# Attention and MoE on one core: q and k of five batches turned by VectorE from doubled rows

## The chip, the core and the metric

The kernel runs on one core of one Trainium2 chip. The metric is the device time of one execution in microseconds (us). Inputs and output are float32 in device memory; the kernel computes with float16 operands and float32 sums. Engines are named as in the profile: PE (TensorE, matmuls), PEld (its weight loads), DVE (VectorE), ACT (ScalarE), POOL (GpSimd, which issues all loads), SP (which issues all stores).

## What is computed

Eight batches, eight heads, 576 tokens, 64 values a head. In the first four heads a token sees itself and the 31 tokens before it. In the last four it sees 32 tokens at distances 0, 4, 8 ... 124. The attention output of all heads, 4608 tokens by 512, then goes through two matrix products with a SiLU between them:

```python
    rel = pos[:, None] - pos[None, :]
    mask_plain = (rel >= 0) & (rel < window)
    mask_dil = (rel >= 0) & (rel < window * dilation) & (rel % dilation == 0)
...
    attn = attn / (np.sum(attn, axis=-1, keepdims=True) + 1e-09)
    return np.matmul(attn, v).astype(np.float32)
...
    h = x @ w_in
    g = h * (1.0 / (1.0 + np.exp(-h)))
    return (g @ w_out).astype(np.float32)
```

with w_in 512 by 2048 and w_out 2048 by 512.

## The kernel before

**Attention of a batch.** The four plain heads are called z=0 here (the prediction says first heads), the four dilated ones z=1 (second heads). In z=1 the tokens are split into four classes (token number modulo 4), and within a class the window is 32 neighbours, so both kinds work on blocks of 32 queries (`QB`) against 64 keys (`KB`): 18 blocks a head in z=0, 4 classes of 5 blocks in z=1.

1. `load_qk` (L113): POOL loads the rows of q and k into tile `n`, turned to float16 on the way: six DMAs a batch from batch 1 on (`load_one`, L97). The tile has two buffers for each of q and k. `load_v` (L120) loads v into `vw` (two buffers) by eight DMAs.
2. `transpose` (L219): PE turns the rows with the identity (L246), so that the 64 values of a head lie on partitions; for one batch 72 transposes in z=0 and 48 in z=1, half of them for k and half for q. They land in PSUM. DVE and ACT copy them into `kT`, `qT` (z=0, L250) and `kC`, `qC` (z=1, L258), which have two buffers each.
3. `scores` (L377): one matmul of 64 rows, 32 query columns as weights and 64 key columns as moving data for each block and head: 72 in z=0 (`score`, L273) and 80 in z=1 (`score_class`, L286). Head h writes partitions 32h to 32h+31 of the result, so four heads use four column groups of the array; the rows are 0 to 63 or 64 to 127. In z=0 the heads 0 to 3 use the row groups 0, 64, 64, 0. In z=1 the row group is the class modulo 2, and the order alternates it within a head, so eight places of the array follow one another. DVE then scales and adds the mask (L304) and takes the row maxima (L371).
4. `exps` (L431): ACT, 64 columns an instruction, with the sum (L451), 18 for z=0 and 20 for z=1.
5. `normal` (L464): DVE multiplies by the reciprocal of the sum into `pn` (L473). `turned` (L477): DVE transposes the probabilities in 32 by 32 blocks (L489); for batch 0 as 32-bit pairs of neighbouring columns, otherwise as 16-bit values.
6. `values` (L530): PE, matmuls of 32 rows with v as weights (L520), then `finish` (L546) copies the result into `xT` (L552, L554).

When pairs are turned, two neighbouring columns stay side by side. So batch 0 orders its keys in another way: `keys` (L263) takes the 64 keys as two halves of 32 and alternates between them, the mask of batch 0 is built in the same order, and `turned_cols` (L491) takes every second column for the product.

**MoE of a batch.** `layer1` (L596): 16 tiles of w_in columns, each 8 matmuls of 288 columns (L602) and a SiLU on ACT (L610). `layer2` (L659): row tiles of 128 tokens, 16 matmuls of 512 columns each (L671), copied by DVE to `ob` (L656, four buffers) and stored by SP. Two batches share nine row tiles: the even batch has four, the odd one five. Batch 0 goes in halves (L627, L647). Results of L602 and L671 lie in the PSUM pool `big`, which has two buffers, taken in turn; transposes, scores and products take the four buffers of the pool `ps`.

**The order** is written by hand. The MoE of batch b is the main line, and `plan_of` (L694) hangs the attention of the next two batches on its steps: steps 0 to 15 stand before the 16 tiles of layer 1, step 16 and each step after it before four matmuls of layer 2, and what is left comes at the end. For b from 2 on: step 0 normalizes batch b+1 z=0, its products are at step 6; step 10 has the scores of (b+1, z=1); step 13 the transposes of (b+2, z=0), step 17 its scores and step 18 its exponentials; step 27 the products of (b+1, z=1); step 31 the transposes of (b+2, z=1). `load_v(b+2)` and `load_qk(b+3)` are issued at step 16, in this order on POOL's queue. Batch 3's transposes stand elsewhere: z=0 at step 17 of b=1, z=1 at steps 1 and 3 of b=2. Each engine runs its own instructions in this order and waits on semaphores.

Of the kernel before, what the change touches and what calls it, by code (L numbers as in the profile page):

```python
# [8 lines left out]
F16 = mybir.dt.float16  # L9
F32 = mybir.dt.float32  # L10
BF16 = mybir.dt.bfloat16
U32 = mybir.dt.uint32
# [4 lines left out]
P = 128  # L17
W = 32
# [4 lines left out]
KB = 2 * QB  # L23
HF = P // 2
URS = (9, 12)


@with_exitstack
def kernel(
# [22 lines left out]
    NS = 512  # L52
    SA = NS // 2
    WM = 12

    ctx.enter_context(tc.manual_schedule())

# [31 lines left out]
    def tiles_qk(b):  # L89

        for which in (0, 1):
            t = nat.tile([P, 2 * sum(URS), D], F16, tag=f"n{which}", name=f"n{which}_{b}")
            u0, u1 = 2 * URS[0], 2 * (URS[0] + URS[1])
            qk[b, 0, which] = t[:, 0:u0].rearrange("p (h u) d -> p h u d", h=2)
            qk[b, 1, which] = t[0 : 2 * UPS[1] if b == 0 else P, u0:u1].rearrange("p (h u) d -> p h u d", h=2)

    def load_one(b, z, which):  # L97
# [8 lines left out]
        for i in (0, 1):  # L106
# [3 lines left out]
                in_=src[b, h : h + 2].rearrange("h (p u) d -> p h (u d)", u=URS[z]),  # L110
            )

    def load_qk(b):  # L113

        tiles_qk(b)
        for z in (1, 0) if b == 1 else (0, 1):
            for which in (1, 0):
                load_one(b, z, which)
# [75 lines left out]
    def build_mask():  # L194

        for n in (1, 2, 3):
            nc.vector.tensor_copy(band[n * W : n * W + W], band[0:W])
        nc.vector.tensor_copy(mask, band[:, None, :].broadcast_to([P, 10, KB]))
        nc.vector.memset(mask[:, 0:3:2, 0:W], NEG)

    first = mask[:, 2:10]

# [3 lines left out]
    def att(b):  # L206
        if b not in state:
            state[b] = {
                "qT": qTs[b % 2],
                "kT": kTs[b % 2],  # L210
                "qC": qCs[b % 2],
                "kC": kCs[b % 2],
                "vw": vws[b % 2],
                "pt": {},
                "xT": xtp.tile([P, HP, S], F16, tag="xT", name=f"xT_{b}"),
            }
        return state[b]

    def transpose(b, z, which, copies):  # L219
# [27 lines left out]
        for i in (0, 1):  # L247
# [3 lines left out]
            else:  # L251
                to_classes(a, which, i, ts[i].rearrange("d (e m) p -> d e m p", m=4), copies[i])

    def to_classes(a, which, i, t, copy):

        e, n = t.shape[1], t.shape[3]
        dst, i0 = ((a["qC"], 0), (a["kC"], W))[which]
        copy(  # L258
            dst[:, 2 * i : 2 * i + 2, :, i0 : i0 + n * e].rearrange("d h r (p e) -> d (h r) p e", e=e),
            t.rearrange("d e m p -> d m p e"),  # L260
        )

    def keys(b, t):  # L263

        return t.rearrange("d (x k) -> d k x", x=2) if b == 0 else t

    def score(b, h, j, dst, start=True):

        a = att(b)
        hp = h // 2  # L270
        o = (h + hp) % 2 * D
        r = slice(o, o + D)
        nc.tensor.matmul(  # L273
            dst[h * QB : h * QB + QB],
            a["qT"][r, hp, j * QB : j * QB + QB],
            keys(b, a["kT"][r, hp, j * QB : j * QB + KB]),
            start=start,
            stop=True,
            skip_group_check=not start,
        )  # L280

    def score_class(b, h, c, j, dst, start=True):

        a = att(b)
        r = slice(c % 2 * D, c % 2 * D + D)
        nc.tensor.matmul(  # L286
            dst[h * QB : h * QB + QB],
            a["qC"][r, h, c // 2, j * QB : j * QB + QB],
            keys(b, a["kC"][r, h, c // 2, j * QB : j * QB + KB]),
            start=start,  # L290
            stop=True,
            skip_group_check=not start,
        )
# [83 lines left out]
    def scores(b, z, half=None):  # L377

        a = att(b)
        if half != 1:
            a["s", z] = (
                [ps.tile([P, 8, KB], F32, tag="ps", name=f"s_{b}_{z}_{m}") for m in (0, 1)],
                [ps.tile([P, 2, KB], F32, tag="ps", name=f"ss_{b}_{z}_{m}") for m in range(1 + z)],
            )
        s, ss = a["s", z]
        n, cut = (NB, 8) if z == 0 else (NC, 3)
        js = range(0 if half != 1 else cut, cut if half == 0 else n)  # L390
        if z:
            for j in js:
                for e in (0, 1):
                    for h in range(HH):
                        for m in (0, 1):
                            dst = s[m][:, 4 * e + j] if j < 4 else ss[m][:, e]
                            score_class(b, h, 2 * e + m, j, dst)
        else:
            for j in js:
                for h in range(HH):  # L400
                    score(b, h, j, (*s, ss[0])[j // 8][:, j % 8])
        ms_ = {None: (0, 1), 0: () if z else (0,), 1: (0, 1) if z else (1,)}[half]
        for m in ms_:
            w = width(b, z, m)
            ms = msp.tile([P, WM, KB], F32, tag="ms", name=f"ms_{b}_{z}_{m}")
            if z:
                f = ms[:, 0:w].rearrange("p (r t) c -> p r t c", t=NC)
                masked(
                    f[:, :, 0:4].rearrange("p r t c -> p r (t c)"),
                    s[m].rearrange("p (r t) c -> p r (t c)", t=4),  # L410
                    first[:, 0:4].rearrange("p t c -> p (t c)")[:, None, :].broadcast_to([P, 2, 4 * KB]),
                )
                masked(f[:, :, 4], ss[m], band_of(2))
            elif m == 0:
                masked(ms[:, 0:8], s[m], first)
            else:
                masked(ms[:, 0:8], s[m], band_of(8))
                masked(ms[:, 8:10], ss[0], band_of(2))
            reduce_max(b, z, m, ms)
# [57 lines left out]
    def turned(b, z, hi):  # L477

        a = att(b)
        w = width(b, z, hi)  # L480
        key = z, hi * (b == 0)
        if key not in a["pt"]:
            a["pt"][key] = ptp.tile([P, DIL * NC, KB], F16, tag="pt", name=f"pt_{b}_{z}_{hi}")
        o = width(b, z, 0) * hi if b else 0
        out = a["pt"][key][:, o : o + w].rearrange("p t c -> p (t c)")
        src = a["pn", z, hi][:, 0:w].rearrange("p t c -> p (t c)")
        if b == 0:
            out, src = out.bitcast(U32), src.bitcast(U32)
        nc.vector.transpose(out, src)  # L489

    def turned_cols(b, pt, at, wd):  # L491

        if b:
            return pt[:, at : at + wd]
        at += at // QB % 2 * (1 - QB)
        if wd == QB:
            return pt[:, at : at + KB - 1 : 2]
        return pt[:, at : at + 2 * (KB - 1)].rearrange("p (t c) -> p t c", t=2)[:, :, 0::2]

    def products(b, z, part, c, j0, j1, dst):  # L500


        a = att(b)
        pt = a["pt"][z, part].rearrange("p t c -> p (t c)")
        o = (c % 2 * 2 + c // 2) * (j1 - j0) * KB
        for kb in range(max(j0 - 1, 0), j1):
            runs = []
            for j in (kb, kb + 1):
                if j0 <= j < j1:
                    key, x, col = dst(j)  # L510
                    at = o + ((j - j0) * 2 + kb - j + 1) * QB
                    if runs and runs[-1][0] == key and runs[-1][2] + QB == col:
                        runs[-1][4] += QB
                    else:
                        runs.append([key, x, col, at, QB])
            n = TL if z and kb == NC - 1 else QB
            for key, x, col, at, wd in runs:
                for h in range(HH):
                    r = slice(h * QB, h * QB + n)
                    nc.tensor.matmul(  # L520
                        x[h // 2][h % 2 * D : h % 2 * D + D, col : col + wd],
                        vws[b % 2][r, NB + kb * DIL + c if z else kb],
                        turned_cols(b, pt[r], at, wd),
                        start=(key, h) not in a["opened"],
                        stop=True,
                        skip_group_check=True,
                    )
                    a["opened"].add((key, h))
# [152 lines left out]

    def transposes(at, b, z, step, copies=both):
        for which in (1, 0):
            at(step, transpose, b, z, which, copies)

    def later(at, b, z, steps, copy=nc.vector.tensor_copy):
# [7 lines left out]
    def plan_of(b):  # L694
        ev = {}

        def at(s, fn, *args):
            ev.setdefault(s, []).append((fn, args))
# [44 lines left out]
        else:  # L743
            if b + 2 < B:
                at(16, load_v, b + 2)
            if b + 1 < B:
                if b == 2:
                    for n in (0, 1):
                        at(1 + 2 * n, transpose, 3, 1, 1 - n, both)
                later(at, b + 1, 0, (0, 0, 4, 6))  # L750
                if b + 3 < B:
                    at(16, load_qk, b + 3)
# [101 lines left out]
```

## Time and profile before

| what | value |
|---|---|
| runs | 315.74, 316.47, 316.49 us; median 316.47 |
| profiled execution | 316.89 us, of which the span from the first to the last instruction is 315.1 |
| DVE, share of the span | 60% |
| ACT | 69% |
| POOL | 24% |
| loads (queue q0) | 36704 packets, 18.61 MB, 45.6% of 16 engines' span |
| stores (queue q1) | 5328 packets, 9.44 MB, 8.2% |
| HBM | 37.21 MB read, 9.44 MB written |

The page gives busy time by engine, the chain of work that ended last, and groups of instructions: line, engine, operation, output and inputs with their shapes, count, then busy us and mean ns of one, then the idle time of the engine before them and what ended it. Busy time of matmuls counts overlapping ones once, so the mean of one (193 ns for a transpose) is far more than what each adds. The chain in order of time and the timeline give start and length of merged pieces; the length of a timeline piece runs to the end of its last instruction, so what a piece costs its engine is read from its start to the start of the next.

### The profile page before, as it was taken

The page shows a single profiled execution, that of the slowest core. Times are in us where ns is not written, and L with a number is a line of the kernel's source. Part 1 is how long each engine was busy: PE and PEld are TensorE (multiplying, and loading weights), DVE is VectorE, ACT ScalarE, POOL GpSimd, SP SyncE. Part 2 cuts the span into 40 slices and gives each one's busy share as a digit, 9 for nine tenths or more (in the row PEclk, how much of TensorE's full clock was granted, in tenths as well). Part 3 has the DMA queues.
Part 4 walks back from the last instruction along what each step waited for, and adds up shares of the span by engine and source line. Part 5 has one row for each costly group of instructions (what it writes and reads, how often), then busy time and mean ns, then how long its engine had stood idle before and what let it go on. Part 6 is the DMA issues. An engine that isn't in the chain of part 4 may idle for free.

```text
span 315.1 us, 11529 instructions
## 1 busy us (share of the span) xinstructions
PE 303.0 (96%) x5051; PEld 193.9 (62%) x5051; DVE 189.4 (60%) x356; ACT 218.6 (69%) x722; POOL 75.7 (24%) x127
## 2 busy tenths in 40 slices
PE   2799999999999999999999999999999999999995
PEld 2468654677446774577644775467745786467544
DVE  2866689445899667875585755883587552730011
ACT  2588688766998569974896568984899458736300
POOL 8826276634005400370008200150000000000000
PEclk9999999999999999999999999999999999999999
DMA  6999999999115921495019900290011100110021
GB/s 113 171 207 208 205 147 196 254 104 139 51 67 102 160 42 36 95 149 92 4 68 139 183 14 2 95 120 4 2 68 36 69 2 3 67 69 0 2 100 67
DMA packets 42081, 28.77 MB, mean 91 GB/s; under 512 B 20928, under 2 KB 37552, under 8 KB 42032
## 3 DMA queue, kind: packets, MB, share of 16 engines
q0 software_dynamic: 36704, 18.61, 45.6%
q1 hardware_dynamic: 5328, 9.44, 8.2%
q8 instruction: 39, 0.64, 0.8%
q14 instruction: 10, 0.08, 0.1%
HBM read 37.21 MB, written 9.44 MB: 148 GB/s over the span
## 4 chain that ended last, share of the span: by engine, by line
PE 88%; ACT 4%; DVE 4%; DMA 2%; issue 1%; POOL 0%; ACTq 0%; POOLq 0%
PE h L602 36%; PE o L671 30%; PE h L627 6%; PE x L520 4%; PE o L647 4%; PE t L246 3%; ACT pe L451 3%; PE s L273 2%; PE s L286 2%; DMA n<-in_q_dram 2%; ACT xT L554 1%; DVE pn L473 1%; DVE ob L656 1%; DVE pt L489 1%; DVE ms L304 0%
## 5 line engine op out<-in xcount | busy, mean ns | idle before, releaser
L602 PE MATMUL h<-xT,w_in 128*128 128x288 f16 x896 | 115.0, 286 | 0.1
L671 PE MATMUL o<-w_out,gT 128*128 128x512 f16 (+1 forms) x528 | 114.6, 373 | 0.0
L610 ACT ACTIVATE gT<-h 128x576 f16<-128x576 f32 x112 | 72.9, 651 | 56.7 <-PE h L602 55.8
L602 PEld LDWEIGHTS <-w_in 128*128 128x128 f16 x896 | 86.0, 98 | 23.9 <-issue 0.6
L671 PEld LDWEIGHTS <-gT 128*128 128x128 f16 x528 | 50.3, 98 | 54.4
L451 ACT ACTIVATE pe<-ms,nm 128x64 f32<-128x64 f32 x246 | 81.6, 335 | 0.1
L656 DVE COPY ob<-o 128x512 f32<-128x512 f32 (+1 forms) x35 | 23.5, 670 | 45.6 <-PE o L671 43.6
L451 ACT ACTIVATION_READ_ACCUMULATOR pe<-ms,nm 128x1 f32 x246 | 46.4, 189 | 0.0
L304 DVE SCALAR_TENSOR_TENSOR ms<-s,mask 128x512 f32<-128x512 f32 x28 | 19.2, 686 | 41.4 <-PE s L286 19.8
L126 POOL DMA_DIRECT2D vw<-in_v_dram x32 | 18.5, 586 | 105.6 <-PE x L520 102.4
L473 DVE TENSOR_TENSOR pn<-pe,r 128x640 f16<-128x640 f32 (+2 forms) x32 | 25.3, 792 | 1.1
L489 DVE STREAM_TRANSPOSE pt<-pn 128x640 f16<-128x640 f16 (+4 forms) x32 | 24.7, 772 | 1.1
L135 POOL DMA_DIRECT2D vw<-in_v_dram x32 | 21.2, 667 | 12.0 <-DMA w_out<-in_moe_w_out_dram 5.7
L371 DVE TENSOR_REDUCE nm<-ms 128x10 f32<-128x640 f32 (+1 forms) x28 | 22.0, 787 | 1.0
L627 PE MATMUL h<-xT,w_in 128*128 128x256 f16 (+1 forms) x128 | 18.3, 300 | 0.0
L520 PEld LDWEIGHTS <-vw 32*64 32x64 f16 (+1 forms) x1264 | 13.1, 107 | 7.7 <-issue 7.2
L554 DVE CAST xT<-x 128x288 f16<-128x288 f32 x24 | 16.3, 826 | 0.0
L520 PE MATMUL x<-pt,vw 32*64 32x64 f16 (+2 forms) x1264 | 15.0, 193 | 1.2 <-DVE pt L489 1.1
L627 PEld LDWEIGHTS <-w_in 128*128 128x128 f16 x128 | 12.7, 103 | 3.7
L647 PE MATMUL o<-w_out,gT 128*128 128x512 f16 x64 | 14.7, 380 | 0.2 <-ACT ob L656 0.2
L246 PEld LDWEIGHTS <-n 64*64 64x64 f16 (+1 forms) x912 | 11.0, 105 | 5.9 <-issue 4.8
L552 DVE CAST xT<-x 128x288 f16<-128x288 f32 x24 | 9.3, 449 | 8.0 <-PE x L520 8.0
(72 smaller groups left out, 224.5 us busy)
## 6 DMA issues: line engine op xcount, KB each, us to landing
out_dram<-ob SPq DMA_DIRECT2D x35, 256.0 KB, 2.0
n<-in_k_dram POOLq DMA_DIRECT2D x9, 288.0 KB, 5.7
n<-in_q_dram POOLq DMA_DIRECT2D x9, 288.0 KB, 6.7
vw<-in_v_dram POOLq DMA_DIRECT2D x31, 80.0 KB, 4.5
vw<-in_v_dram POOLq DMA_DIRECT2D x32, 72.0 KB, 4.1
w_in<-in_moe_w_in_dram POOLq DMA_DIRECT2D x4, 512.0 KB, 9.8
w_out<-in_moe_w_out_dram POOLq DMA_DIRECT2D x4, 512.0 KB, 11.1
n<-in_k_dram POOLq DMA_DIRECT2D x14, 144.0 KB, 7.2
```

The lines of the kernel that those rows point to most:

```text
L135: nc.gpsimd.dma_start(out=vw[h * QB : h * QB + QB, 0:NB], in_=v[b, h].rearrange("(m p) d -> p m d", p=QB))
L371: nc.vector.tensor_reduce(out=nm[:, 0:w], in_=ms[:, 0:w], axis=AX.X, op=ALU.max, negate=True)
L451: nc.scalar.activation(pe[:, t, :], src[t], AF.Exp, bias=a["nm", z, hi][:, t : t + 1], scale=k, accum_out=l[:, t : t + 1],)
L473: nc.vector.tensor_tensor(pn[:, 0:w], a["pe", z, hi][:, 0:w], r[:, 0:w, None].broadcast_to([P, w, KB]), ALU.mult)
L489: nc.vector.transpose(out, src)
L520: nc.tensor.matmul(x[h // 2][h % 2 * D : h % 2 * D + D, col : col + wd], vws[b % 2][r, NB + kb * DIL + c if z else kb], turned_cols(b, pt[ ...
L602: nc.tensor.matmul(h[:, half, 0:HS], w_in16[:, c, f * P : f * P + P], xT[:, c, half * HS : half * HS + HS], start=(c == cs[0]), stop=(c == ...
L610: nc.scalar.activation(gT[:, f, s0 : s0 + S].rearrange("p (a c) -> p a c", a=2), h[:, :, 0:HS], AF.Silu)
L627: nc.tensor.matmul(hs[i // m][:, i % m, 0 : c1 - c0], w_in16[:, c, (f + i) * P : (f + i + 1) * P], xT[:, c, c0:c1], start=(c == 0), stop=( ...
L647: nc.tensor.matmul(o, gT[:, f, t * P : (t + 1) * P], w_out16[:, f, :], start=(f == 0), stop=(f == NFF - 1),)
L656: copy(ob, o)
L671: nc.tensor.matmul(o[:, 0, 0:m], gT[:, f, t * P : (t + 1) * P], w_out16[:, f, cols], start=(f == 0), stop=(f == NFF - 1),)
```

## The change

From batch 3 on (`DT = 3`) q and k no longer go through PE. POOL loads them in blocks of 32 rows on 32 partitions: for z=0's q each row is a token, 32 values at a time; for the others each row is a pair of neighbouring tokens, of which 96 values are taken. A second copy, 32 columns on in device memory, goes to the next 32 partitions, and the other two heads to the upper 64 partitions: four DMAs for each of k z=0, q z=0, k z=1, q z=1. DVE turns each of the four in one instruction of 1152 16-bit values a partition (`turn_qk`), straight into the tiles `qT`, `kT`, `qC`, `kC`, where even and odd tokens now lie in two planes. The calls stand at the steps where the transposes of that batch stood; both of (3, z=1) are at step 1 of b=2.

The scores of these batches read through `turned_q` and `turned_k`. The row group is now that of the head (0 for heads 0 and 1, 64 for 2 and 3), and the heads follow in the order 0, 2, 1, 3; in z=1 the class is the outer loop.

The probabilities of all batches are turned as 32-bit pairs. Therefore all batches take their keys alternating between two halves, the mask in SBUF is built in that order, and all products read every second column.

The transposes of batches 1 and 2 stay on PE.

```diff
+DT = 3
...
-        nc.vector.tensor_copy(mask, band[:, None, :].broadcast_to([P, 10, KB]))
-        nc.vector.memset(mask[:, 0:3:2, 0:W], NEG)
+        pairs = mask.rearrange("p t (k x) -> p t k x", x=2)
+        nc.vector.tensor_copy(
+            pairs, band.rearrange("p (x k) -> p k x", x=2)[:, None].broadcast_to([P, 10, W, 2])
+        )
+        nc.vector.memset(pairs[:, 0:3:2, :, 0], NEG)
...
     def load_qk(b):
 
         tiles_qk(b)
+        if b >= DT:
+            for z in (0, 1):
+                for which in (1, 0):
+                    u, e = (1, QB) if z == which == 0 else (2, GW)
+                    n = HH // 2 * S // u // QB
+                    for half in (0, 1):
+                        for x in (0, 1):
+                            o = half * HF + x * QB
+                            nc.gpsimd.dma_start(
+                                out=turned_rows(b, which, z)[o : o + QB],
+                                in_=bass.AP(
+                                    (q, k)[which].tensor,
+                                    (b * H + z * HH + half * HH // 2) * S * D + x * QB,
+                                    [[u * D, QB], [u * QB * D, n], [1, e]],
+                                ),
+                            )
+            return
...
+    def turn_qk(b, z, which):
+        n = HH // 2 * MG
+        if which == 0 and z == 0:
+            nc.vector.transpose(
+                att(b)["qT"].rearrange("p a c -> p (a c)"), turned_rows(b, 0, 0).rearrange("p g t -> p (g t)")
+            )
+            return
+        o = which * (1 + z) * QB
+        src = turned_rows(b, which, z)
+        nc.vector.transpose(
+            planes(b, z, which)[:, :, o : o + n * QB].rearrange("p r (g t) -> p r g t", t=QB),
+            src.rearrange("p g (r t) -> p r g t", t=QB)[:, 0:3:2],
+        )
...
     def keys(b, t):
 
-        return t.rearrange("d (x k) -> d k x", x=2) if b == 0 else t
+        return t.rearrange("d (x k) -> d k x", x=2)
+
+    def turned_q(b, z, h, c, j):
+        r = slice(h // 2 * D, h // 2 * D + D)
+        if z == 0:
+            return att(b)["qT"].rearrange("p a c -> p (a c)")[r, h % 2 * S + j * QB : h % 2 * S + j * QB + QB]
+        o = h % 2 * HS + j * KB + c // 2
+        return planes(b, 1, 0)[r, c % 2, o : o + KB - 1 : 2]
+
+    def turned_k(b, z, h, c, j):
+        r = slice(h // 2 * D, h // 2 * D + D)
+        if z == 0:
+            o = h % 2 * HS + (j + 1) * QB // 2
+            return planes(b, 0, 1)[r, :, o : o + QB].rearrange("p r (x t) -> p t r x", x=2)
+        o = h % 2 * HS + j * KB
+        t = planes(b, 1, 1)[r, c % 2, o : o + 2 * KB].rearrange("p (x t y) -> p y t x", x=2, y=2)
+        return t[:, c // 2]
...
-                for e in (0, 1):
-                    for h in range(HH):
-                        for m in (0, 1):
-                            dst = s[m][:, 4 * e + j] if j < 4 else ss[m][:, e]
-                            score_class(b, h, 2 * e + m, j, dst)
+                for c, h in [(c, h) for c in range(DIL) for h in (0, 2, 1, 3)] if b >= DT else [
+                    (2 * e + m, h) for e in (0, 1) for h in range(HH) for m in (0, 1)
+                ]:
+                    e, m = c // 2, c % 2
+                    score_class(b, h, c, j, s[m][:, 4 * e + j] if j < 4 else ss[m][:, e])
...
-                for h in range(HH):
+                for h in (0, 2, 1, 3) if b >= DT else range(HH):
...
-        if b == 0:
-            out, src = out.bitcast(U32), src.bitcast(U32)
-        nc.vector.transpose(out, src)
+        nc.vector.transpose(out.bitcast(U32), src.bitcast(U32))
...
         for which in (1, 0):
+            if b >= DT:
+                at(step, turn_qk, b, z, which)
+                continue
             at(step, transpose, b, z, which, copies)
...
                 if b == 2:
-                    for n in (0, 1):
-                        at(1 + 2 * n, transpose, 3, 1, 1 - n, both)
+                    transposes(at, 3, 1, 1)
```

`planes` splits the tile into the two planes of even and odd tokens; `turned_rows` finds the loaded rows in tile `n`.

More of the change, by code (lines that the diff above doesn't have):

```diff
@@ L54 @@
     WM = 12
+    MG = S // KB
+    GW = 3 * QB
     ctx.enter_context(tc.manual_schedule())
@@ L91, in tiles_qk @@
         for which in (0, 1):
-            t = nat.tile([P, 2 * sum(URS), D], F16, tag=f"n{which}", name=f"n{which}_{b}")
+            t = nat.tile([P, H // 2 * MG * GW], F16, tag=f"n{which}", name=f"n{which}_{b}")
+            if b >= DT:
+                qk[b, which] = t
+                continue
+            t = t[:, 0 : 2 * sum(URS) * D].rearrange("p (u d) -> p u d", d=D)
             u0, u1 = 2 * URS[0], 2 * (URS[0] + URS[1])
@@ L111, in load_one, with turned_rows @@
             )
+    def turned_rows(b, which, z):
+        t, n = qk[b, which], HH // 2 * MG
+        if which:
+            return t[:, z * n * GW : (z + 1) * n * GW].rearrange("p (g e) -> p g e", e=GW)
+        if z == 0:
+            return t[:, 0 : n * KB].rearrange("p (g e) -> p g e", e=QB)
+        return t[:, n * KB : n * (KB + GW)].rearrange("p (g e) -> p g e", e=GW)
     def load_qk(b):
         tiles_qk(b)
+        if b >= DT:
[15 more added lines that the diff above has]
+            return
         for z in (1, 0) if b == 1 else (0, 1):
@@ L252, in transpose, with planes @@
                 to_classes(a, which, i, ts[i].rearrange("d (e m) p -> d e m p", m=4), copies[i])
+    def planes(b, z, which):
+        t = att(b)[(("qT", "kT"), ("qC", "kC"))[z][which]]
+        t = t.rearrange("p a c -> p (a c)") if z == 0 else t.rearrange("p a x c -> p (a x c)")
+        n = HH // 2 * MG * QB + (which * QB if z == 0 else (QB, 3 * QB)[which])
+        return t[:, 0 : 2 * n].rearrange("p (r c) -> p r c", r=2)
+    def turn_qk(b, z, which):
[11 more added lines that the diff above has]
+        )
     def to_classes(a, which, i, t, copy):
@@ L263, in keys @@
     def keys(b, t):
-        return t.rearrange("d (x k) -> d k x", x=2) if b == 0 else t
+        return t.rearrange("d (x k) -> d k x", x=2)
[7 more added lines that the diff above has]
+        r = slice(h // 2 * D, h // 2 * D + D)
+        if z == 0:
+            o = h % 2 * HS + (j + 1) * QB // 2
[3 more added lines that the diff above has]
+        return t[:, c // 2]
     def score(b, h, j, dst, start=True):
@@ L274, in score @@
             dst[h * QB : h * QB + QB],
-            a["qT"][r, hp, j * QB : j * QB + QB],
-            keys(b, a["kT"][r, hp, j * QB : j * QB + KB]),
+            turned_q(b, 0, h, 0, j) if b >= DT else a["qT"][r, hp, j * QB : j * QB + QB],
+            turned_k(b, 0, h, 0, j) if b >= DT else keys(b, a["kT"][r, hp, j * QB : j * QB + KB]),
             start=start,
@@ L287, in score_class @@
             dst[h * QB : h * QB + QB],
-            a["qC"][r, h, c // 2, j * QB : j * QB + QB],
-            keys(b, a["kC"][r, h, c // 2, j * QB : j * QB + KB]),
+            turned_q(b, 1, h, c, j) if b >= DT else a["qC"][r, h, c // 2, j * QB : j * QB + QB],
+            turned_k(b, 1, h, c, j) if b >= DT else keys(b, a["kC"][r, h, c // 2, j * QB : j * QB + KB]),
             start=start,
@@ L486, in turned, with turned_cols @@
         src = a["pn", z, hi][:, 0:w].rearrange("p t c -> p (t c)")
-        if b == 0:
-            out, src = out.bitcast(U32), src.bitcast(U32)
[L489 to L494, printed above, removed]
+        nc.vector.transpose(out.bitcast(U32), src.bitcast(U32))
+    def turned_cols(pt, at, wd):
         at += at // QB % 2 * (1 - QB)
@@ L522, in products @@
                         vws[b % 2][r, NB + kb * DIL + c if z else kb],
-                        turned_cols(b, pt[r], at, wd),
+                        turned_cols(pt[r], at, wd),
                         start=(key, h) not in a["opened"],
@@ L683, in transposes @@
         for which in (1, 0):
+            if b >= DT:
+                at(step, turn_qk, b, z, which)
+                continue
             at(step, transpose, b, z, which, copies)
```

## Prediction

> **What bounds the kernel now.** I read the page first, for the bound.
>
> ```profile
> PE 303.0 (96%) x5051; PEld 193.9 (62%) x5051; DVE 189.4 (60%) x356; ACT 218.6 (69%) x722; POOL 75.7 (24%) x127
> ...
> PE 88%; ACT 4%; DVE 4%; DMA 2%; issue 1%; POOL 0%; ACTq 0%; POOLq 0%
> ...
> L489 DVE STREAM_TRANSPOSE pt<-pn 128x640 f16<-128x640 f16 (+4 forms) x32 | 24.7, 772 | 1.1
> ...
> L246 PE MATMUL t<-ident,n 64*64 64x64 f16 (+1 forms) x912 | 13.2, 193 | 0.6 <-DMA n<-in_q_dram 0.4 <-issue 0.3
> ```
>
> That is the page: busy time by engine, the chain that ended last by engine, and two groups. TensorE (PE) is busy 96% of the span and 88% of the chain that ended last; from 20 us on it hardly idles. So each instruction that leaves PE shortens the run by its place in PE's sequence, and work added to DVE, ACT or POOL costs nothing until PE waits for it. Next the chain in order of time (start, us, line, count), for prices of such places:
>
> ```profile
> 111.75 3.04 PE h L602 x24
> 114.80 0.76 PE t L246 x72
> 115.56 3.04 PE h L602 x24
> ...
> 130.58 2.70 PE o L671 x12
> 133.28 0.70 PE t L246 x48
> 133.98 0.97 PE o L671 x4
> ...
> 257.56 6.00 PE h L602 x48
> ...
> 275.24 3.56 PE o L671 x16
> ```
>
> The 72 transposes split 48 matmuls of L602: 111.75 to 118.60 is 6.85 us, and the unbroken 48 took 6.00. They cost 0.85 us: their own 0.76, and the drain of one more change of matmul shape. In the same way 48 transposes cost 4.37 - 3.56 = 0.81.
>
> **Off PE: transposes of batches 3 to 7.** 600 of the 912. Batches 4 to 7 lose 0.85 + 0.81 each: 6.64. Batch 3's stand elsewhere: 77.62 to 82.35 is 4.73 us for 16 L671 and 72 transposes, and 16 without a break take 3.46 (275.17 to 278.63 in the timeline): 1.27. 99.20 to 106.20 is 7.00 for 48 L602 and two groups, against 5.88 in another batch: 1.12. Sum **-9.03 us**. The copies behind them (L250, L258; 0.75 us each on DVE, 0.64 on ACT) go too; PE does not wait for them, so that is room, not time.
>
> **Pairs in the transpose of the probabilities.**
>
> The groups with their shapes kept apart show both kinds (busy us, then mean ns):
>
> ```profile
> L489 DVE STREAM_TRANSPOSE pt<-pn 128x640 f16<-128x640 f16 x21 | 17.8, 845 | 0.7
> ...
> L489 DVE STREAM_TRANSPOSE pt<-pn 128x320 uint32<-128x320 uint32 x1 | 0.5, 511 | 0.0
> ```
>
> 640 halves (f16 values) turned as 320 pairs save 0.33 us each, 512 save 0.27 (711 to 445 ns). Three products (L520) on PE wait for this result, by their length against the same product elsewhere: 1.08 against 0.78 at 89.98, 0.96 against 0.81 at 96.34, 1.34 against 0.81 at 273.83. The first two go whole, since DVE has saved 0.60 and 1.27 us by then; of the third go the 0.33 us of its last transpose: **-0.78**. The products now read every second column; batch 0 does that already at full clock (24.96 to 27.9 us), in bunches of four every 31.6 ns, as at 164.6 without the step. Cost 0, and no bound to keep, since the trace shows the operation itself.
>
> **Added on DVE: four transposes of 1152 halves a batch.** No row has that size. The line through 512 (711 ns) and 640 (845) gives 1.38 us. Below, the pair rate gives 0.78 for 576 pairs; above, the slowest strided row of DVE, L554 with 826 ns for 288 elements, gives 3.3. I take 1.38: same operation, same type. Per batch DVE gets 4 x 1.38 - 4 x 0.75 - 1.27 = +1.25 us of about 36; the question is only where.
> - Step 13 (first heads): DVE ends the row maxima at 149.9 in batch 3's stage; two turns, 1.31 from start to start, end at 152.5. PE wants them for the scores at 154.22 - 0.87 = 153.35. Cost 0, cover 0.8 us.
> - Step 17 of batch 1: 77.83 + 2.6 = 80.4, wanted at 81.1. Cost 0. Step 1 of batch 2 ends ahead of the xT copies at 106.66. Cost 0.
> - Step 31 of batches with four row tiles (2 and 4) has no cover. DVE's timeline, start and us first:
>
> ```profile
> 130.42 2.72 DVE L554 CAST xT<-x 128x288 f16<-128x288 f32 x4
> 133.72 0.76 DVE L258 COPY kC<-t 128x576 f16<-128x576 f16 x1 [0.58 <-PE t L246]
> 134.39 0.75 DVE L258 COPY qC<-t 128x576 f16<-128x576 f16 x1
> 135.05 0.68 DVE L656 COPY ob<-o 128x512 f32<-128x512 f32 x1
> ```
>
> The output copy at 135.05 frees the PSUM buffer that the next batch's second L602 tile needs (`big` has two). Today it ends at 135.73 and PE gets there at 135.95. Changed: turns 133.07 to 135.69, the copy ends at 136.38, while PE gets there at 134.07 + 0.98 = 135.05. PE stands still for about 1.38 us, in two batches: **+2.75**. Batches 3 and 5 have a fifth row tile in the other buffer, 3.45 us of cover.
>
> **Loads.** A batch's q and k come by 16 DMAs of 576 or 1152 pieces (64 or 192 bytes written) in place of six: 11520 packets. The nearest rows are v's pieces of 128 bytes; the DMA view of 66 to 68 us, which holds almost only these, says
>
> ```profile
> DMA packets 1911, 0.25 MB, mean 123 GB/s; under 512 B 1888, under 2 KB 1911, under 8 KB 1911
> ```
>
> 955 packets a us, so a load takes 12 us. It is issued behind v from 100 us on and wanted at 149.6 (first heads) and 168. POOL issues for 16 x 0.66 us, and the next batch's v, queued behind, has 40 us. Output stores on SP's queue share the engines, but their four buffers are 3.4 us apart. Cost 0. The other bound is the rate of the old loads with 1152-byte packets, 161 a us (1771 in 104 to 115): too slow, see the rivals; 955 is nearer by size.
>
> **Scores.** This is the open term. Every key operand now alternates between columns 32 to 128 bytes apart (batch 0 already does), in batches 1 and 2 too. Batch 0 ran before 22.7 us, where 128x256 matmuls start every 213 ns and afterwards every 109: half clock, though the clock column prints 1.00 there.
>
> ```profile
> 10.27 0.70 PE L246 MATMUL t<-ident,n 64*64 64x64 f16 x36 [0.36 <-DMA n<-in_q_dram]
> ...
> 17.02 0.81 PE L273 MATMUL s<-kT,qT 64*32 64x64 f16 x40
> ...
> 18.72 0.61 PE L520 MATMUL x<-pt,vw 32*64 32x64 f16 x32
> ```
>
> That is the timeline of PE (start, us, line, count). All three stream 64 columns in bunches of four. By their single starts, a bunch takes 53.3 ns in the first (plain) and the third (step of two), and 61.7 in the scores. So the alternation already binds at half clock. At full clock a plain score bunch takes 29.3 ns. If the limit is a time of the memory, a bunch stays at 61.7; if it is 74 PE cycles against 64, it is some 33, as fast as instructions now arrive (8.2 ns each). More than 61.7 is unlikely: a faster PE doesn't slow the memory. I take 61.7, since a limit outside PE explains why a step of two costs nothing. First heads: 18 bunches + 0.12 of start = 1.23 us against 0.71, in seven batches: 3.64. Second heads: the new order (0, 2, 1, 3) cycles four places of the array instead of eight, so in batches 3 to 7 20 bunches + 0.12 = 1.35 against 0.74: 3.05; in 1 and 2 eight overlap and 61.7 is hidden by arrival (66). **+6.7**.
> The Trainium skill (Advanced Engine Details and Errata, SBUF Cachelines) speaks against this change: two consecutive reads must hit one 16-byte line to reach full rate. Read as halving the rate, it gives 58.7 ns a bunch and a sum 0.7 us lower than mine; no row at full clock shows it.
> The skill (TensorEngine Tiling, PSUM Pressure) also says that two row groups cannot write one PSUM bank at once, which the new order does. The first heads do it today, starting 3 ns apart; the trace disagrees.
>
> The mask's two operations at 28 us (0.49 us, at most 0.8) meet an idle DVE: 0.
>
> **Sum:** -9.03 - 0.78 + 2.75 + 6.7 = -0.36 us. The profiled run took 316.89 us (span 315.1), 0.42 above the median of 316.47; against that median the forecast is **316.1**.
>
> **Rivals.**
> - *The alternation costs cycles, not time.* Scores +0, sum -7.06: 309.4. For it: both clocks would show 10 extra cycles. Against: they appear only with the far step. 0.22; something between, near 312.8, 0.06.
> - *The turns are late* (slower). If 1152 halves over two planes take 2.0 us instead of 1.38, the standstill grows by 1.24 twice and step 13 loses its 0.8 us of cover and 0.45 more in four batches: +4.3, 320.4. It decides from about 1.7 us a turn. For it: DVE is nearly full from 82 to 106. Against: the runs are 32 halves long. 0.12.
> - *The loads come late.* From 100 us to the last turn of first heads, due at 221, POOL's queue has 36096 packets to move; below 298 a us PE waits. At 250 it would be 23 us late: 339. Against: 955 measured. 0.05.
> - *It does not do what it says* (transposes stay on PE): excluded by PE's instruction list, 1200 rows shorter.
>
> **Numbers.** Forecast 0.55. Its terms: scores 4.8 (a bunch of 53.3 ns, the plain one at half clock) to 6.7, standstill 0.4 (turns of 0.78) to 4.1 (turns of 1.7); both ends together give 311.9 and 317.4, its own range, with less of the low end, is 313.5 to 317.5. The likeliest case lies close to no change, and 0.3% (0.95 us) is what a measurement can tell: it splits 0.19 faster, 0.26 same, 0.10 slower. With the rivals: faster 0.47, same 0.26, slower 0.27. The range 309.0 to 318.5 leaves out the late turns and the late loads, and perhaps a tenth of the first rival's cases.
>
> **What would show it.** L246 falls from 912 to 312. The bunches of the score lines are the test: 72 scores near 1.2 us (this), near 0.7 (first rival). PE stands still near 135 and 208 us for the output copy. A turn's mean is 1.3 to 1.5 us. No DVE wait for a load. I am wrong if PE waits for DVE or POOL at the scores.

## The result and the profile after

| | before | changed |
|---|---|---|
| median, us | 316.48 (315.74 to 316.96, 4 runs) | 321.33 (320.87 to 322.13, 4 runs) |
| profiled execution, us (span) | 316.89 (315.1) | 320.87 (319.1) |

The ratio is 1.0158, 95% interval 1.013 to 1.0187: the change made the kernel slower, by some 4.9 us. The forecast was 316.1, its range 309.0 to 318.5.

The page of the changed kernel: busy time by engine, and the chain that ended last by engine.

```profile
PE 305.0 (96%) x4451; PEld 197.3 (62%) x4451; DVE 190.5 (60%) x354; ACT 208.3 (65%) x704; POOL 112.6 (35%) x177
...
PE 88%; DVE 5%; ACT 3%; DMA 2%; issue 1%; POOL 1%; DVEq 0%; POOLq 0%
```

PE has 600 matmuls fewer and is busy 2 us longer. So the instructions went, and the ones that stayed became dearer. The groups by line say which were asked of whom: PE's transposes, then DVE's new ones (busy us, mean ns).

```profile
L282 PE MATMUL t<-ident,n 64*64 64x64 f16 (+1 forms) x312 | 4.7, 201 | 1.1 <-DMA n<-in_q_dram 1.1
```

```profile
L309 DVE STREAM_TRANSPOSE kC<-n 128x1152 f16<-128x1152 f16 x5 | 6.9, 1379 | 0.0
...
L303 DVE STREAM_TRANSPOSE qT<-n 128x1152 f16<-128x1152 f16 x5 | 6.7, 1334 | 0.0
```

912 transposes became 312, and a turn takes 1.33 to 1.38 us: both as forecast. The chain (start, us, line, count) shows what did not come out. Before, the scores of the second heads of batch 3 and of the first heads of batch 4 stood there so:

```profile
111.00 0.61 PE s L286 x64
...
119.46 0.63 PE s L273 x64
```

The same stretch in the changed kernel, where the last 16 and the last 8 matmuls of a group have lines of their own:

```profile
110.95 1.21 PE s L364 x64
112.16 0.28 PE ss L364 x16
112.44 5.99 PE h L676 x48
...
119.29 1.88 PE s L351 x61
121.17 0.22 PE ss L351 x7
```

The 48 matmuls of layer 1 now run unbroken in 5.99 us (6.85 before): the gain is there. But from their first start to the start of what follows, the second heads' scores take 1.49 us (0.75 before; 1.35 forecast), and the first heads' 2.10 (0.71 before; 1.23 forecast). By single starts (of the single matmuls in the trace), a bunch of four first-head matmuls takes 111 ns; 18 bunches are 2.0 us.

The other loss forecast, the late output copy, is in DVE's timeline (start, us), and in PE's line behind it:

```profile
134.16 1.39 DVE L309 STREAM_TRANSPOSE kC<-n 128x1152 f16<-128x1152 f16 x1
135.47 1.33 DVE L309 STREAM_TRANSPOSE qC<-n 128x1152 f16<-128x1152 f16 x1
136.73 0.65 DVE L730 COPY ob<-o 128x512 f32<-128x512 f32 x1
```

```profile
137.43 5.06 PE L676 MATMUL h<-xT,w_in 128*128 128x288 f16 x40 [1.09 <-DVE ob L730]
```

The two turns stand ahead of the copy, and PE waits for it. From start to start PE loses 1.25 us here and 0.90 at 211, in the same place of a later batch, where the profile names ACT's gT as what it waited for. At 100.7 PE loses 0.27 us to an output copy that has the xT copies ahead of it, and no turn.

### The profile page after: what moved, and what is told of

It reads as the page before. It is cut to its first block, busy times and chain, and to the rows that moved or that the text cites. A ratio compares the mean times of both kernels' runs of the same rounds, so it can differ in the third digit from the quotient of the medians.

```text
span 319.1 us, 10398 instructions
## 1 busy us (share of the span) xinstructions
PE 305.0 (96%) x4451; PEld 197.3 (62%) x4451; DVE 190.5 (60%) x354; ACT 208.3 (65%) x704; POOL 112.6 (35%) x177
## 4 chain that ended last, share of the span: by engine, by line
PE 88%; DVE 5%; ACT 3%; DMA 2%; issue 1%; POOL 1%; DVEq 0%; POOLq 0%
PE h L676 34%; PE o L745 33%; PE s L351 4%; PE o L721 4%; PE h L701 3%; PE x L594 3%; PE s L364 2%; DMA n<-in_q_dram 2%; ACT pe L529 2%; DVE xT L628 1%; PE t L282 1%; ACT xT L628 1%; DVE ob L730 1%; POOL n L108 1%; DVE pn L551 1%
## 5 line engine op out<-in xcount | busy, mean ns | idle before, releaser
L676 PEld LDWEIGHTS <-w_in 128*128 128x128 f16 x896 | 86.4, 98 | 26.6 <-issue 2.7
L140 POOL DMA_DIRECT2D n<-in_q_dram x40 | 29.5, 765 | 1.1 <-PE x L594 0.8
L140 POOL DMA_DIRECT2D n<-in_k_dram x40 | 26.4, 683 | 6.6 <-DMA n<-in_k_dram 3.8
L701 PE MATMUL h<-xT,w_in 128*128 128x256 f16 (+1 forms) x128 | 17.3, 289 | 0.0
L628 DVE CAST xT<-x 128x288 f16<-128x288 f32 x24 | 16.3, 825 | 0.3 <-PE x L594 0.3
L565 DVE STREAM_TRANSPOSE pt<-pn 128x320 uint32<-128x320 uint32 (+2 forms) x32 | 15.8, 495 | 1.1
L351 PEld LDWEIGHTS <-qT 64*32 64x32 f16 x576 | 12.8, 104 | 4.4 <-issue 3.3
```

The source lines that it names most:

```text
L140: nc.gpsimd.dma_start(out=turned_rows(b, which, z)[o : o + QB], in_=bass.AP((q, k)[which].tensor, (b * H + z * HH + half * HH // 2) * S * ...
L351: nc.tensor.matmul(dst[h * QB : h * QB + QB], turned_q(b, 0, h, 0, j) if b >= DT else a["qT"][r, hp, j * QB : j * QB + QB], turned_k(b, 0, ...
L628: copy(a["xT"][:, 2 + hp].rearrange("d (i r) -> d r i", r=DIL)[:, 2 * e : 2 * e + 2], x.rearrange("d (r i) -> d r i", r=2)[:, :, 0:CL],)
L676: nc.tensor.matmul(h[:, half, 0:HS], w_in16[:, c, f * P : f * P + P], xT[:, c, half * HS : half * HS + HS], start=(c == cs[0]), stop=(c == ...
L701: nc.tensor.matmul(hs[i // m][:, i % m, 0 : c1 - c0], w_in16[:, c, (f + i) * P : (f + i + 1) * P], xT[:, c, c0:c1], start=(c == 0), stop=( ...
```

## The experiments

**Theory:** the loss lies in the order in which a score matmul reads its 64 key columns; the turned layout of k makes that order worse than the two-place alternation that I had priced. In batches 3 to 7 the first heads' tokens lie in two planes (even and odd tokens, 1216 bytes apart), and each plane gives two places 32 bytes apart, so one matmul takes its columns in turn from four places (stretches of memory that it reads on from), `[2,2,16]`, where batch 0 cycles through two, `[2,32]`. **Rivals:** the third level of the pattern costs, whatever it reads; the long distance costs; or PE waits for something else, such as the turned rows.

### Nine orders of the same reads (key_orders)

```diff
+            t = planes(b, 0, 1)[r, :, o : o + QB]
+            flat = att(b)["kT"].rearrange("p a c -> p (a c)")[r, o : o + KB]
+            if b == 3:
+                return t.rearrange("p r (x t) -> p r t x", x=2)
+            if b == 4:
+                return t.rearrange("p r (x t) -> p x r t", x=2)
+            if b == 5:
+                return t.rearrange("p r t -> p t r")
+            if b == 6:
+                return flat.rearrange("p (a t) -> p t a", a=4)
+            return flat.rearrange("p (x t y) -> p t x y", x=2, y=2)
```

(These are the first heads of batches 3 to 7; other orders stand likewise in batches 1 and 2 and for the second heads of batches 4 to 7.)

> Only the order changes in which the scores read their 64 key columns, another one in each batch (the keys then no longer meet the mask, so the output is not the attention's). First heads, 72 matmuls: batch 1 swaps neighbours two columns apart, batch 2 cycles eight places 16 bytes apart, batch 3 alternates two places 32 bytes apart under a third level, batch 4 reads runs of 16 under a third level, batch 5 alternates the two halves 1216 bytes apart in two levels, batch 6 cycles four places 32 bytes apart in two levels, batch 7 alternates two places 64 bytes apart after two adjacent columns each. Changed kernel: 2.09 us in batches 3 to 7 (four places, three levels, 32 and 1216 bytes apart), 1.21 in batches 1 and 2 (two places). Theory 'places' (the number of places cycled sets the price): batch 3 1.23, batch 4 0.7, batch 5 1.23, batch 6 2.1, batch 7 0.7 to 1.23, batch 1 0.7, batch 2 2.1 or more. Rival 'levels' (a third level of the pattern sets it): batches 3, 4 and 7 2.1, batches 5, 6 and 2 1.23. Rival 'distance' (the 1216 bytes set it): batches 3, 6, 7 at most 1.23, batch 4 about 0.8, batch 5 2.1. Second heads, 80 matmuls, 1.49 in the changed kernel: batch 4 without alternation (step of two), batch 5 with query columns side by side, batch 6 with both plain, batch 7 with the heads in the order 0 to 3. If the key order sets their price too, batches 4 and 6 take 0.75 and 5 and 7 1.49; if the query's step of two adds the part above 1.35, batch 5 takes 1.35.

The chain's lines of the scores (start, us; first heads L371, second heads L384; the last 8 or 16 matmuls of a group have lines of their own, 0.07 to 0.28 us, left out here, and some records are missing from the counts):

```profile
67.08 1.88 PE s L371 x64
...
82.30 1.10 PE s L371 x58
...
118.75 0.63 PE s L371 x64
...
145.36 0.61 PE s L384 x61
...
152.96 1.10 PE s L371 x64
...
182.29 1.21 PE s L384 x62
190.62 1.89 PE s L371 x54
...
225.88 0.67 PE s L371 x64
```

In order of time: batch 2 (eight places), 3 (two places, three levels), 4 (runs of 16, three levels), the second heads of 4 (no alternation), 5 (two places 1216 bytes apart), the second heads of 5 (query side by side), 6 (four places, two levels), 7 (two places in runs of two). The whole groups take 2.11, 1.23, 0.71, 0.75, 1.23, 1.49, 2.11 and 0.75 us. Batch 1, which swaps neighbours inside 8 bytes, keeps 29 ns a bunch. So neither the levels (1.23 and 0.71 with three, 2.11 with two) nor the distance (32 or 1216 bytes: 1.23) sets the price. With one column at each visit the number of places does: one place takes 29 ns a bunch, two 62, four and eight 111; with two columns at each visit two places take 36 (batch 7). The query's step and the order of the heads (batch 7's second heads, 1.49) cost nothing. With these reads the profiled run took 315.2 us.

### One plane for the first heads' keys (key_rows)

```diff
-                    u, e = (1, QB) if z == which == 0 else (2, GW)
+                    u, e = (2, GW) if z else (1, QB)
...
-            return planes(b, 0, 1)[r, :, o : o + QB].rearrange("p r (x t) -> p t r x", x=2)
+            return keys(b, att(b)["kT"].rearrange("p a c -> p (a c)")[r, o : o + KB])
```

> The first heads' k of batches 3 to 7 is loaded like their q, one token in a piece of 32 values, so that their keys lie in one plane and the scores alternate between two places instead of four; 1152 pieces more in each such load. Theory 'places' or 'distance': 72 scores fall from 2.09 to 1.23 us in five batches, 4.3 us, 317.0 against 321.3. If the four places are not what costs (a wait of another kind, such as PE waiting for the turned rows), no change: 321.3. If more pieces make loads late: slower than 321.3.

317.50 us, 1.0032 [1.0019, 1.0045] against before; 3.8 below the changed kernel, where 4.3 was expected. The line that answers to 1.88:

```profile
119.20 1.09 PE s L350 x64
```

So four places instead of two cost the change nearly 4 us in the time of the whole run too. Of the half microsecond that is missing, 0.35 is the second standstill, 1.25 us here (at 208) in place of 0.90; the added pieces of load cost nothing that shows.

### Each half of the change alone (plain_keys, pairs_only)

plain_keys has DVE's turns, the loads of key_rows, and keys in order (its main lines):

```diff
-        return t.rearrange("d (x k) -> d k x", x=2)
+        return t.rearrange("d (x k) -> d k x", x=2) if b == 0 else t
...
-        nc.vector.transpose(out.bitcast(U32), src.bitcast(U32))
+        if b == 0:
+            out, src = out.bitcast(U32), src.bitcast(U32)
+        nc.vector.transpose(out, src)
```

> As the run with one plane, and all key operands but batch 0's are read in order again (a step of two in the second heads of batches 3 to 7), so the probabilities of batches 1 to 7 are turned as halves. It is the first part of the change alone, without the pairs. Theory that the alternation is the loss: first heads 0.71 in seven batches, second heads 0.75: from 321.3 down by 6.9 (batches 3 to 7) + 1.0 (1 and 2) + 3.8 (second heads) and up by 0.8 for the three waits on the turned probabilities: 310.4, below both kernels. Rival that DVE becomes the bound, now that it has both the turns and the slower transposes (1.4 us a batch more): 314 or more, with PE waiting for DVE at 90 to 100 us.

pairs_only is the changed kernel with `DT = 8`:

> The second part alone: q and k of all batches are turned by PE as before, the probabilities as pairs, and all keys alternate between two places. First heads 1.21 in seven batches against 0.71 (+3.5), second heads 0.80 against 0.74 (+0.4), three waits on the turned probabilities gone (-0.8): 316.5 + 3.1 = 319.6 by the theory that the alternation is the loss; 315.7 if only the turned layout's keys lose.

plain_keys: 310.84 us, 0.9821 [0.9807, 0.9836]. pairs_only: 319.28, 1.0087 [1.0067, 1.0107]. The turns of q and k alone are a gain of 5.5 us; the pairs alone a loss of 2.9, since the transposes that they shorten are DVE's, off the path but for 0.8 us, while the order that they force on the keys is paid by PE. The first heads' scores of batch 4 in plain_keys, without their last 8:

```profile
117.31 0.63 PE s L346 x64
```

and in pairs_only, behind the second heads' of batch 3 without their last 16:

```profile
111.75 0.67 PE s L364 x64
...
120.27 1.09 PE s L351 x60
```

The 80 scores of the second heads take 0.81 us in pairs_only, with keys from two places, and 0.75 in plain_keys, with keys in order and the new order of heads; with both they take 1.49. By single starts, pairs_only has eight matmuls on eight places of the array side by side in 62 to 66 ns; the changed kernel, whose layout has one row group for each head, has four in 69. So 0.68 of the 0.74 us that the second heads lose comes from the two together: slower reads, and half as many of them at a time.

DVE, busy 199.0 us in plain_keys, did not become the bound.

### The late output copy (moved, plain_moved, plain_moved_b2)

```diff
-                if b == 2:
-                    transposes(at, 3, 1, 1)
+                transposes(at, b + 1, 1, 5)
...
-            if b + 2 < B:
-                transposes(at, b + 2, 1, 31)
```

> The changed kernel with the second heads' turns of batches 3 to 7 taken from step 31 (step 1 of batch 2's stage for batch 3) to step 5 of the stage that uses them, behind the output copies and ahead of 4 us in which DVE idles. Theory that the two turns ahead of the output copy hold PE up: the standstills of 1.25 and 0.90 us and a wait of 0.27 at 100.7 go, 321.3 - 2.4 = 318.9. Rival, the wait only moves (PE then waits at the second heads' scores, about 147 us, for the turns): 320.5 to 321.5.

319.24 us (1.0102 [1.0079, 1.0125] against before). PE now goes from one layer into the other without a break at the place that answers to 137.43:

```profile
132.15 3.56 PE o L745 x16
135.71 5.88 PE h L676 x48
```

Of the expected 2.4 us 2.1 came (1.9 when each kernel is taken against the kernel before in its own measurement); the wait of 0.27 us at 101 stayed, so it belongs to the output copy behind the xT copies there and not to the turns.

With the keys in order as well:

> Keys in order and probabilities as halves, as in the run of that kind (310.8), and the second heads' turns at step 5 as well. Standstills there 1.25 and 1.25 and a wait of 0.27: 310.8 - 2.8 = 308.0 if they go; 310 or more if DVE, which turns the probabilities more slowly here, is late for the scores at 147 us.

308.25 us, 0.9749 [0.9735, 0.9764]. And with `DT = 2`:

> The same, and batch 2 is turned by DVE too, so that PE is left with the 192 transposes of batches 0 and 1 in place of 312. Its transposes take 0.76 and 0.70 us of PE with about 0.1 for each break: 1.6 us less, 306.4, if the loads of batch 2, issued in the first 35 us beside the weights, come in time; slower than 308 if PE waits for them between 62 and 75 us.

306.92 us, 0.9711 [0.9696, 0.9725]: the best of all, 9.4 us below before and 14.4 below the changed kernel. It is half a microsecond short of what was expected, and PE shows why (start, us):

```profile
72.25 0.68 PE L359 MATMUL s<-kC,qC 64*32 64x64 f16 x64 [0.37 <-DVE qC L305]
```

Batch 2's last load lands at 69.6 us by the chain, and its turns and then PE wait for it.

### Steps and runs (key_orders_2, key_orders_3)

What is it about a place? In key_orders_2 the first heads read with plain steps, in key_orders_3 in visits of two and four adjacent columns and with steps of 3 and 6 (of both the main lines; two more batches of key_orders_2 alternate inside small groups):

```diff
+                m = {3: 4, 4: 8, 5: 16}[b]
+                return flat[r, o : o + m * (KB - 1) + 1 : m]
...
+            x, y = {3: (4, 2), 4: (2, 4), 7: (4, 4)}[b]
+            return flat[r, o : o + KB].rearrange("p (x t y) -> p t x y", x=x, y=y)
```

> Again only the order of the first heads' 64 key columns differs from the changed kernel (the output is not the attention's). No alternation: batch 3 a step of 4 columns (8 bytes), batch 4 of 8 (16 bytes), batch 5 of 16 (32 bytes). Alternation of two places inside small groups: batch 6 8 bytes apart, batch 7 16 bytes apart. Batch 1 two places 128 bytes apart, each with a step of two; batch 2 the same with a step of one. Theory 'lines': a read is cheap only if the one before or after it lies in the same few bytes, wherever it goes next: the steps of 8 and 16 cost what four places do, 2.1 us for 72 scores, the step of 4 between 0.7 and 1.23, alternation at 8 bytes 0.7 and at 16 bytes 1.23. Rival 'jumps': only going back and forth between places costs, a long step forward does not: 0.7 for all three steps, 1.23 for both alternations. The second heads' bunch of 69 ns against 62: if the step of two inside two places makes it, batch 1 takes 0.12 us more than batch 2.

> Only the order of the first heads' 64 key columns differs from the changed kernel (the output is not the attention's). Alternation in runs: batch 3 four places 32 bytes apart, two adjacent columns in each visit; batch 4 two places 64 bytes apart, four adjacent columns; batch 7 four places, four adjacent columns. Plain steps: batch 5 of 3 columns (6 bytes), batch 6 of 6 (12 bytes). Seen so far, in ns a bunch of four matmuls of 64 columns: in order or a step of two 29, a step of four 61, of eight and sixteen 116 to 118; two places 62, four or eight 111; two places in runs of two 36. Theory 'every change of 16-byte line is paid' (1.8 ns): steps of 3 and 6: 24 and 48 lines, 44 and 88; runs of two over four places 32 visits, 59; runs of four 16 visits, 29. Rival 'pairs are enough' (what counts is that each read has one neighbour in its line, the number of places does not matter then): runs of two over four places 36 and runs of four 29; steps as above.

The times, 318.85 and 316.58 us in one execution each, tell nothing by themselves, since each batch has another order. Chain of key_orders_2, batches 3, 4 and 5 (steps of 4, 8 and 16 columns):

```profile
82.55 1.08 PE s L363 x60
...
118.99 1.94 PE s L363 x59
...
155.40 1.99 PE s L363 x53
```

Chain of key_orders_3, batches 3 (four places, visits of two), 4 (two places, visits of four), 5 and 6 (steps of 3 and 6):

```profile
82.87 1.06 PE s L357 x64
...
119.31 0.63 PE s L357 x64
...
154.25 0.85 PE s L357 x60
...
191.62 1.49 PE s L357 x51
```

Per bunch of four matmuls, by single starts; a line is a stretch of 16 bytes, that is eight columns, and the second column of the table counts how often a matmul passes from one line to another:

| order of the 64 columns | changes of 16-byte line | 1.8 ns each | measured, ns |
|---|---|---|---|
| step 1 or 2 | 8 or 16 | 14 or 29 | 29 |
| step 3 | 24 | 43 | 46 |
| step 4 | 32 | 58 | 61 |
| step 6 | 48 | 86 | 87 |
| step 8, step 16 | 64 | 115 | 116, 118 |
| four or eight places | 64 | 115 | 111 |
| four places, visits of two | 32 | 58 | 60 |
| four places, visits of four | 16 | 29 | 30 |
| two places | 64 | 115 | 62 |
| two places, visits of two | 32 | 58 | 36 |
| places 8 bytes apart, group in one line | 8 | 14 | 28 |
| the same, group 4 or 12 bytes into a line | 24 | 43 | 42 to 44 |
| the same, group 8 bytes into a line | 56 | 101 | 58 to 59 |

The 1.8 ns are 116 ns by 64 changes. Plain steps fit "1.8 ns for each change of a 16-byte line, and never below 29 ns a bunch" within 3 ns; four and more places fit it within 4. The rival that a long step is free and only going back costs is out (steps of 8 and 16), and so is the one that pairs suffice (four places, visits of two). Just two places cost about half of it. Why is open: if two lines were kept, a line would serve all its eight reads and the bunch would take 29 ns; no run looked further.

The last three rows are batch 6 of key_orders_2, which alternates inside groups of 16 bytes. Each bunch there begins 4 bytes further on than the one before, and by single starts the bunches take 28, 44, 59 and 44 ns in turn, again and again. So the lines have fixed ends: the same order of columns is free where the group lies in one line, and where it lies half in each of two neighbouring lines it costs nearly what two distant places do (58 ns and 62). Batch 7 there, 16 bytes apart, took 55 to 62 ns.

Two places with a step of two (batch 1 there) took 69 ns against 62, and 1.46 us against 1.33: that is the second heads' part above the forecast, which reads just so.

## Why the prediction was wrong, step by step

| step | forecast, us | in the changed kernel's trace |
|---|---|---|
| transposes off PE | -9.03 | as forecast where it can be read off: 6.85 to 5.99 and 4.37 to 3.56 in a batch; plain_moved, which has no other large term, is 8.1 below before, where -9.03 and its wait of 0.27 give 8.8 |
| products no longer wait | -0.78 | -0.8: the first two gone, -0.34 at the last one (1.34 to 1.00) |
| PE stands for the output copy | +2.75 | +2.42 (1.25, 0.90, 0.27); the forecast's own times give 1.33 each (136.38 - 135.05), not 1.38 |
| first heads' scores | +3.64 | +8.0 (1.39 in five batches, 0.51 and 0.57 in batches 2 and 1) |
| second heads' scores | +3.05 | +4.0 (0.74 in five batches, 0.25 in the other two together) |
| loads, mask, products with a step | 0 | 0 |
| sum | -0.36 | +4.6 by these rows; the spans differ by 4.0, the medians by 4.85 |

**The step that failed** is the sentence "Every key operand now alternates between columns 32 to 128 bytes apart (batch 0 already does), in batches 1 and 2 too." Batch 0 alternates between two places; the first heads of batches 3 to 7 cycle through four, which the diff says in one line (the planes in the pattern of `turned_k`). I gave them batch 0's bunch of 61.7 ns, and called more "unlikely" because I asked only whether a faster PE could slow the memory, not whether the memory was asked the same thing. 111 - 62 = 49 ns a bunch, 18 bunches, five batches: 4.4 of the 5.2 us by which the forecast was short. Another 0.7, 0.14 us in five batches, is the same mistake in small: the second heads' keys now step by two as well.

**What held.** The open term was rightly named and its mechanism rightly chosen: two places take 62 ns at the full clock, as they did at half of it, so the price is a time and not PE cycles, and the rival at 309.4 fell. That the second heads' loss comes with the change from eight places of the array to four held too: on eight, in batches 1 and 2, they lose 0.25 us together. Turns (1.33 to 1.38 us) and their place in DVE's order came as worked out. The two standstills came where they were forecast and went when the turns were moved; in the second, shorter one the profile names ACT's gT and not the copy, and why is open. Late loads and late turns did not come; a batch's load took some 12.5 us (11585 packets from 107.0 to 119.5), near the 12 of the forecast. The range failed with the same term: its upper bound held the bunch at 61.7, and no rival had a worse layout of the keys.

**A rule on the order of reads.** The Trainium skill (Advanced Engine Details and Errata, SBUF Cachelines) says that at least two hits on a 16-byte line are needed to hide the memory's latency, and that a different line for each access is penalized. The runs agree on the line. They show that two hits are not enough here: a step of four, with two reads in each line, still takes twice the time (61 ns), and four reads in a row bring it to 29. With a single read in each line it is not half the rate but a quarter (111 to 118). So the estimate from it, 58.7 ns, fitted two places by the number and missed four.
The other rule of the Trainium skill that was weighed (TensorEngine Tiling (Array Packing), Gotcha 1: PSUM Pressure), that different row tiles cannot access the same PSUM bank at once, did not bind: with keys in order the new order of heads takes 0.75 us for the second heads (plain_keys), as the old one did.

## What to carry to other kernels

When PE is the bound, count in which order its small matmuls read memory, matmul by matmul and for every batch: a layout that takes work off PE or another engine can make each of them two to four times as long (62 and 111 ns for 29 here). Price a new pattern by a row with the same number of places and the same number of columns at each visit, not by one that is merely also strided; where there is none, work out the time with a new line for each column as well, the slowest order measured here (111 to 118 ns). And a part that frees an engine off the path (here the pairs) has nothing to pay with if it touches the operands of the one that is on it: alone it lost 2.9 us, while the other part without it won 5.5.

## What the runs showed of the hardware

Not expected: the price of the reading order follows the changes of 16-byte lines (table above), 1.8 ns for a bunch of four matmuls, two of them on the same rows; matmuls on eight places of the array pay side by side (62 to 66 ns for eight in batches 1 and 2, 62 for four); a third level in the pattern and a jump of 1216 bytes cost nothing of themselves (29 and 62 ns with three levels, 62 with the jump); two places are dealt with at about half the price (62 ns for 115 by the rule).
